# Weight blocks, outer sums and the first layer of the odd batches in a cross-attention and gated-MLP kernel

## The chip, the cores and the metric

The kernel runs on one core of one Trainium2 chip. A core has TensorE (PE; its weight loads are listed as PEld), VectorE (DVE), ScalarE (ACT), GpSimd (POOL) and SyncE (SP), which here issues most DMA transfers. The metric is the device time of one execution in microseconds (us), lower is better; a change is judged by the median of several runs.

## The reference

For each of 8 batches and 8 heads, 512 tokens read 32 state rows by softmax attention, and the state rows read the tokens the same way. The results are concatenated over the 544 rows, the heads are joined to rows of 512 features, and a gated MLP follows, with h times cos(h) as its gate.

```
scores = scale * x @ state.T;   a  = softmax(scores);    xread = a  @ state
scores2 = scale * state @ x.T;  a2 = softmax(scores2);   sread = a2 @ x
rows = concat([xread, sread], axis=2)  ->  (8*544, 512)
h = rows @ w_in          # w_in  512 x 2048
out = (h * cos(h)) @ w_out   # w_out 2048 x 512
```

The weights of the MLP are given in double precision and are turned to float32 on the chip.

## The kernel before

**Steps.** The work is written as one list of steps, and every engine's instructions follow that order. A step is one tile of 128 of the 2048 hidden features for the 512 tokens of one batch: 16 steps a batch, 128 steps for the token rows, then 16 for the state rows of all batches. Two batches are a pair of 32 steps. A step has a phase: 0 and 1 are the first and last eight tiles of the even batch, 2 and 3 those of the odd one.

**First layer.** The kernel never forms `xread`. It multiplies the state by the weights first (L329, kept by ACT as `sw`, L462) and then by the softmax weights `aT`. `hidden` (L491) does it for one tile with two matmuls of 512 columns. From batch 2 on two tiles are taken together, and in phases 0 to 2 the 2 x 2 blocks of the pair are multiplied with seven products of 256 columns instead of eight (`seven_part`, L541). For that POOL makes four sums of `sw` blocks (`sw_sums`, L524) three steps ahead, DVE makes four half sums of `aT` once a batch (`halves`, L510), ACT copies two partial results (L544, L545), and DVE adds two halves afterwards (`seven_sum`, L550). Which tiles take this form is decided in `seven` (L501).

**Gate.** ACT rounds h to whole turns (`gate`, L561), DVE takes the distance (`gate2`, L564), ACT the sine (`gate3`, L567), DVE the product (`gate4`, L581), which writes g into one of twelve buffers ("quads") of four tiles in `g_all`. A quad is taken from the front of a list and put at its end when it is free.

**Second layer.** Each pair of batches against both halves of `w_out` is again seven products (`Product`, L710), and each product is seven stages of four matmuls (L760). A stage reads one 128 x 512 weight block out of a ring of four, which SP fills from DRAM (`fetch_block`, L698). The sums of g that the seven products need are the outer sums (L707 from `outer_sum`, step numbers in a table, L1085), the sums inside a product are POOL's (`Product.sums`, also L707). The first pair's even batch is an exception: it is multiplied with the plain weights in SBUF.

**First pair.** Steps 0 to 31 also convert the weights (ACT L244 and L247, DVE L250 and L253, POOL L258), run the second batch's attention, and make the weight blocks: `w_out` is four matrices a11, a12, a21, a22. Three outer weight sums (L1105 on DVE, L1148 on POOL) form the other matrices, four POOL sums of quarters per matrix (`inner_weights`, L674) form its blocks, and 8 blocks per matrix are stored to `blocks_kept` (L678): the four quarters themselves ("raw") and four sums. a22's own blocks are not made there: the matrix is copied to a DRAM tile `kept` in four transfers (L1110, step 17), fetched back at steps 41 to 44, and its sums and stores follow at steps 46 to 50; a12's at steps 51 to 55 (`late_weights`).

Of the kernel before, what the change touches and what calls it, by code (L numbers as in the profile page):

```python
# [22 lines left out]
def kernel(  # L23
# [67 lines left out]
    kept = spare.tile([QT, P, S], F32)  # L91
# [409 lines left out]
    def seven(t):  # L501
        return t.pair is not None and t.b > 1 and t.phase < 3
# [161 lines left out]
    def inner_weights(which, m, temps, pieces=range(4), at_step=None):  # L664
# [11 lines left out]
        def send(i):  # L676
            block = (m11, m12, m22, m21, t4, t1, t2, t3)[i]
            nc.sync.dma_start(  # L678
                out=blocks_kept[which, (0, 1, 3, 7, 2, 4, 5, 6)[i]].rearrange(
                    "p (i d) -> p i d", d=P),  # L680
                in_=block)

        if at_step is None:
            for i in range(4 if 3 in pieces else 0):
                send(i)
                stores_due.append(lambda i=i: send(4 + i))
        else:
            for i in range(8):
                weights_at[at_step + (i + 1) // 2].append(
                    lambda i=i: send(i))  # L690
# [366 lines left out]
    stage_at, sums_at, outer_at, weights_at = [defaultdict(list)  # L1057
                                               for _ in range(4)]
# [26 lines left out]
    for n in range(B // 2):  # L1085
        end = n == B // 2 - 1
        for r, engine, o, x1, x2, half in (
                ((25, 26), dve, 0, 2, 0, 0),
                ((27 - (not n), 28 - (not n)), dve, 0, 2, 0, 1), ((31, 31), pool, 2, 3, 2, 0), ((33, 33), dve, 0, 3, 0, 0),
# [4 lines left out]
            for i in range(2):  # L1094
                outer_at[PERIOD * n + r[i]].append(
                    (engine, n, o, x1, x2, half, i))
# [10 lines left out]
    def move(to_dram, q, i):  # L1107
        sb = quad(q)[:, i]
        o, x = (kept[i], sb) if to_dram else (sb, kept[i])
        nc.sync.dma_start(out=o, in_=x)  # L1110

    late_quads = []

    def late_weights(step):
        if step == 41:
            late_quads.append(quads_free.pop(0))
        if step < 45:
            move(False, late_quads[0], step - 41)
        if step == 46:
            late_quads.append(quads_free.pop(0))  # L1120
            inner_weights(2, matrix(late_quads[0]), quad(late_quads[1]),
                          at_step=step)
        elif step == 51:
            quads_free.append(late_quads[0])
            inner_weights(1, a12, quad(late_quads[1]), at_step=step)
        elif step == 56:
            quads_free.extend([A12, late_quads[1]])
# [17 lines left out]
    def pool_sum():  # L1145
        for i in range(QT):
            o, x1, x2 = [quad(q)[:, i] for q in (SQ, A21, A22)]
            nc.gpsimd.tensor_tensor(o, x1, x2, op=ALU.add)  # L1148

    for at_, what in (  # L1150
            (15, lambda: quads_free.append(10)),
            (16, pool_sum),
            (17, lambda: quads_free.append(9)),
            (17, lambda: inner_weights(3, matrix(SQ), temps[1])),
            (20, lambda: inner_weights(5, matrix(A21), temps[0])),
            (23, lambda: inner_weights(4, matrix(A22), temps[1])),
            (23, lambda: quads_free.append(A11)),
            (25, lambda: quads_free.append(A21)),
            (25, lambda: inner_weights(6, matrix(SQ), temps[0])),
# [4 lines left out]
    for step in (41, 42, 43, 44, 46, 51, 56):  # L1164
# [21 lines left out]
    def first_pair(step, t):  # L1186
# [13 lines left out]
        else:  # L1200
# [9 lines left out]
            go(3)  # L1210
            if step == 1:
# [9 lines left out]
        gate4(t)  # L1221
        if last >= 0 and 4 < step < 11:
# [3 lines left out]
        if step == 6:  # L1226
            states_kept(1, side_banks[0])
# [133 lines left out]
```

## Time and profile before

| | |
|---|---|
| median of 12 runs | 760.3 us (757.62 to 761.71) |
| the profiled execution | 759.69 us, of which the span is 757.9 us |
| granted TensorE clock in it | 0.993 |
| PE waited longest for | DVE's gate product at L491: 11.7 us in 10 waits |
| SP waited longest for | PE's L760 before a ring fetch: 302.0 us in 128 waits |
| largest groups | POOL L707 337.5 us, PE L760 344.9 us, PE L491 110.4 us |

A row of the timeline has start, duration, engine, line, operation, written tile, read tiles, the number of instructions, and in brackets the idle time before them and what ended it. An fp32 matmul appears as two records. Line numbers are those of the kernel before.

### The profile page before, as it was taken

To read this page: it belongs to the slowest core of one execution; us is meant where nothing else is said; L and a number is where in the kernel's file an instruction comes from. 1 tells how busy PE (TensorE), PEld (TensorE's weight loads), DVE (VectorE), ACT (ScalarE), POOL (GpSimd) and SP (SyncE) were. 2 spreads that over 40 slices of the span, in tenths; PEclk is the share of its full clock that TensorE was granted. 3 is DMA by queue.
4 is the path that set the end of the run, shared out by engine and by line. 5 is a ranking of instruction groups with operands and counts; after the bars stand their busy time and mean duration, and the time that the engine had idled before them with its cause. 6 is when DMAs were issued, how large, how long until landed. Compare 5 with 4: busy or idle time off the path is not lost.

```text
span 757.9 us, 10478 instructions
## 1 busy us (share of the span) xinstructions
PE 721.4 (95%) x3552; PEld 507.3 (67%) x3552; DVE 493.7 (65%) x685; ACT 330.4 (44%) x538; POOL 514.5 (68%) x476
## 2 busy tenths in 40 slices
PE   8999889789999989999999999999999999999998
PEld 3443323347777866677768776677778767888886
DVE  5768789785974647676867666859746446264650
ACT  3877963634363435344454454443634432211110
POOL 2343477676998975387998853579989534799600
PEclk9999999999999999999999999999999999999999
DMA  8595479767235894576326843672324456445661
GB/s 249 167 268 176 154 167 305 249 148 173 83 96 135 183 263 157 112 155 139 87 67 143 181 107 89 146 173 81 85 69 112 122 171 151 114 153 177 182 158 40
DMA packets 211509, 113.42 MB, mean 150 GB/s; under 512 B 158400, under 2 KB 173248, under 8 KB 211456
## 3 DMA queue, kind: packets, MB, share of 16 engines
q1 hardware_dynamic: 210368, 112.23, 57.2%
q8 instruction: 28, 0.46, 0.3%
q10 hardware_dynamic: 960, 0.39, 0.2%
q14 instruction: 25, 0.20, 0.1%
q0 software_dynamic: 128, 0.13, 0.1%
HBM read 88.08 MB, written 24.64 MB: 149 GB/s over the span
## 4 chain that ended last, share of the span: by engine, by line
PE 55%; POOL 18%; DVE 2%; issue 2%; DMA 1%; ACT 1%; POOLq 0%; DVEq 0%
PE o L760 30%; POOL g_all L707 14%; PE h L491 9%; PE h L541 9%; PE at L861 2%; PE at L329 2%; POOL swS_all L524 2%; POOL sw L524 1%; PE at L426 1%; DMA g_all<-blocks_kept 1%; PE o L861 1%; DVE g_all L707 1%; DVE xT L311 1%; DVE q_all L564 0%; ACT q_all L567 0%
## 5 line engine op out<-in xcount | busy, mean ns | idle before, releaser
L707 POOL TENSOR_TENSOR g_all<-g_all 128x512 f32<-128x512 f32 x256 | 337.5, 1350 | 109.8 <-PE o L760 62.6
L760 PE MATMUL o<-g_all 128*128 128x256 f32 x1456 | 344.9, 382 | 4.8 <-DMA g_all<-blocks_kept 2.4
L760 PEld LDWEIGHTS o<-g_all 128*128 128x128 f32 x1456 | 273.7, 190 | 65.8 <-issue 15.3
L491 PE MATMUL h<-aT,sw 128*128 128x512 f32 x224 | 110.4, 617 | 12.4 <-DVE g_all L581 11.7
L564 DVE TENSOR_TENSOR q_all<-q_all,h 128x1024 f32<-128x1024 int32 (+1 forms) x88 | 85.4, 971 | 51.4 <-ACT q_all L561 51.3
L567 ACT ACTIVATE q_all<-q_all,halfpi 128x1024 f32<-128x1024 f32 (+1 forms) x88 | 84.1, 956 | 64.0 <-DVE q_all L564 63.9
L581 DVE TENSOR_TENSOR g_all<-h,q_all 128x1024 f32<-128x1024 f32 (+1 forms) x88 | 85.8, 975 | 39.3 <-ACT q_all L567 37.1
L561 ACT ACTIVATE q_all<-h 128x1024 int32<-128x1024 f32 (+1 forms) x88 | 73.2, 831 | 67.3 <-DVE g_all L581 34.2
L491 PEld LDWEIGHTS h<-aT,sw 128*128 128x128 f32 x224 | 41.6, 193 | 59.4 <-issue 31.8
L550 DVE TENSOR_TENSOR h<-h,sums_all 128x256 f32<-128x256 f32 x72 | 30.9, 429 | 63.0 <-PE h L541 48.3
L707 DVE TENSOR_TENSOR g_all<-g_all 128x1024 f32<-128x1024 f32 x40 | 56.9, 1439 | 0.1
L541 PE MATMUL h<-aS_all,swS_all 128*128 128x256 f32 x144 | 45.8, 400 | 3.0 <-ACT sums_all L545 1.8
L541 PE MATMUL h<-aT,sw 128*128 128x256 f32 x144 | 45.2, 396 | 3.3 <-DVE g_all L581 2.9
L765 ACT COPY o<-o 128x256 f32<-128x256 f32 x26 | 9.3, 357 | 86.6 <-PE o L760 86.6
L258 POOL TENSOR_TENSOR w_in<-w_in,aS_all 128x1024 int32<-128x1024 int32 (+1 forms) x10 | 19.3, 1929 | 39.1 <-DVE w_in L253 23.7
L541 PE MATMUL h<-aS_all,sw 128*128 128x256 f32 x144 | 43.6, 384 | 0.0
L771 ACT COPY o<-sums_all 128x256 f32<-128x256 f32 x26 | 9.8, 377 | 74.2 <-PE o L760 74.2
L604 DVE SCALAR_TENSOR_TENSOR held<-o,held 128x512 f32<-128x512 f32 x40 | 27.1, 681 | 21.3 <-PE o L760 20.8
L541 PEld LDWEIGHTS h<-aS_all,swS_all 128*128 128x128 f32 x144 | 25.6, 191 | 22.5 <-POOL g_all L707 8.3
L462 ACT COPY sw<-at 128x512 f32<-128x512 f32 x50 | 26.8, 588 | 31.2 <-PE at L329 31.2
L258 POOL TENSOR_TENSOR g_all<-g_all,aS_all 128x1024 int32<-128x1024 int32 x8 | 18.9, 2366 | 23.6 <-DVE g_all L253 11.2
L541 PEld LDWEIGHTS h<-aT,sw 128*128 128x128 f32 x144 | 26.2, 191 | 13.1 <-DVE g_all L581 9.8
(115 smaller groups left out, 878.9 us busy)
## 6 DMA issues: line engine op xcount, KB each, us to landing
g_all<-blocks_kept SPq DMA_DIRECT2D x202, 256.0 KB, 2.8
blocks_kept<-g_all SPq DMA_DIRECT2D x48, 256.0 KB, 3.4
g_all<-in_moe_w_out_dram SPq DMA_DIRECT2D x8, 1024.0 KB, 5.0
out_dram<-ot SPq DMA_DIRECT2D x128, 64.0 KB, 2.2
g_all<-in_moe_w_in_dram SPq DMA_DIRECT2D x6, 1024.0 KB, 5.3
xT<-in_x_dram SPq DMA_DIRECT2D x96, 64.0 KB, 3.0
x_b<-in_x_dram SPq DMA_DIRECT2D x24, 256.0 KB, 4.8
x_b<-in_x_dram SPq DMA_DIRECT2D x16, 128.0 KB, 4.4
```

What stands on the lines that cost most here:

```text
L258: nc.gpsimd.tensor_tensor(bits, bits, e, op=ALU.add)
L462: (copy or nc.scalar.copy)(sw_of[self.b, nt][:, j, c0:c1], to[j][:, c0:c1])
L491: nc.tensor.matmul(out=t.hp, lhsT=t.lhs(i), rhs=t.rhs(i), start=(i == 0), stop=(i == t.kn - 1))
L541: nc.tensor.matmul(out=out_, lhsT=w, rhs=r, start=start, stop=True, skip_group_check=True)
L550: nc.vector.tensor_tensor(o, h2[:, LO], sums_all[:, 0], op=ALU.add)
L561: nc.scalar.activation(t.q.bitcast(I32), t.hp, func=ACTF.Copy, bias=0.25)
L564: nc.vector.tensor_tensor(t.q, t.q.bitcast(I32), t.hp, op=ALU.subtract)
L567: nc.scalar.activation(t.q, t.q, func=ACTF.Sin, bias=halfpi, scale=-TWO_PI)
L581: nc.vector.tensor_tensor(g, t.hp, t.q, op=ALU.mult)
L604: nc.vector.scalar_tensor_tensor(out=out.t[:, ch], in0=bank, scalar=TWO_PI, in1=b.t[:, ch], op0=ALU.mult, op1=ALU.add)
L707: engine.tensor_tensor(o[:, i:i + n], x1[:, i:i + n], x2[:, i:i + n], op=ALU.subtract)
L760: nc.tensor.matmul(out=o, lhsT=ring[(self.first + k) % NB][:, i], rhs=g[:, i], start=(start and i == 0), stop=(i == QT - 1), skip_group_ch ...
```

## The change

1. `seven` has no bound on the phase any more: the last eight tiles of batches 3, 5 and 7 take the seven-product form.
2. The four POOL sums of a11's quarters go from steps 12 to 15 to steps 7 to 10. Raw blocks and sums are stored apart (`send_raw` and `send`); a11's raw blocks go at step 15, its sums at step 16.
3. The third outer weight sum, a22's place from the second sum minus a11, goes from DVE (steps 20 and 22) to POOL (step 18, four instructions). The fourth, DVE's, goes from steps 23 and 24 to 22 and 25.
4. a22's raw blocks are stored at step 17 in their final place, in place of the four copies to `kept`, and a12's at step 19. Step 41 fetches a22's four raw blocks at once; the late sums and stores, now four stores per matrix, begin at steps 45 and 52.
5. The outer sums of the first pair stand at steps 25, 26, 26 and 28 (before: 25, 26, 26, 27), and the first two of them between the distance and the gate product. The half sums for batch 2 stand in the same place at steps 29 and 30.
6. At step 6 the kept state rows (L172) come before a weight conversion.

```diff
     def seven(t):
-        return t.pair is not None and t.b > 1 and t.phase < 3
+        return t.pair is not None and t.b > 1
...
+    def send_raw(which, m, back=False):
+        for i, block in zip((0, 1, 7, 3), quarters(m)):
+            o, x = blocks_of(which, i), block
+            nc.sync.dma_start(out=x if back else o, in_=o if back else x)
...
-                ((27 - (not n), 28 - (not n)), dve, 0, 2, 0, 1), ...
+                ((27 - (not n), 28), dve, 0, 2, 0, 1), ...
...
+                at_ = mid_at if n == 0 and r[i] < 27 and r[0] == 25 else outer_at
...
         if step == 41:
             late_quads.append(quads_free.pop(0))
-        if step < 45:
-            move(False, late_quads[0], step - 41)
-        if step == 46:
+            send_raw(2, matrix(late_quads[0]), back=True)
+        elif step == 45:
             late_quads.append(quads_free.pop(0))
             inner_weights(2, matrix(late_quads[0]), quad(late_quads[1]),
-                          at_step=step)
-        elif step == 51:
+                          send_at=(49, 49, 50, 51))
+        elif step == 52:
...
-        weights_at[12 + i].append(lambda i=i: inner_weights(
-            0, a11, temps[0], (i,)))
-        weights_at[17].append(lambda i=i: move(True, A22, i))
+        weights_at[7 + i].append(lambda i=i: inner_weights(
+            0, a11, temps[0], (i,), () if i < 3 else (16,) * 4))
...
-            ((20, 22), A22, SQ, A11, ALU.subtract),
-            ((23, 24), SQ, A12, A22, ALU.subtract)):
+            ((22, 25), SQ, A12, A22, ALU.subtract)):
...
+            (15, lambda: send_raw(0, a11)),
+            (17, lambda: send_raw(2, a22)),
+            (19, lambda: send_raw(1, a12)),
...
+            (18, lambda: pool_sum(A22, SQ, A11, ALU.subtract)),
...
+            for what in mid_at[step]:
+                outer_sum(*what)
...
+        if step == 6:
+            states_kept(1, side_banks[0])
         if last >= 0 and 4 < step < 11:
             convert(last, "bcdf")
...
+        if t.b == 1 and s in (13, 14):
+            halves(2, s - 13)
```

On POOL in steps 5 to 18 of the kernel before, L258 are the conversions, L674 the sums of quarters and L1148 the first outer weight sum:

```order
L258 TENSOR_TENSOR g_all<-g_all,aS_all 128x1024 x3
L674 TENSOR_TENSOR g_all<-g_all 128x512
L258 TENSOR_TENSOR g_all<-g_all,aS_all 128x1024
L674 TENSOR_TENSOR g_all<-g_all 128x512
L258 TENSOR_TENSOR g_all<-g_all,aS_all 128x1024
L674 TENSOR_TENSOR g_all<-g_all 128x512
L258 TENSOR_TENSOR g_all<-g_all,aS_all 128x1024
L674 TENSOR_TENSOR g_all<-g_all 128x512
L1148 TENSOR_TENSOR g_all<-g_all 128x512 x4
```

In the changed kernel the same place reads as follows (L257 the conversions, L681 the sums of quarters, L1144 the two outer weight sums on POOL):

```order
L681 TENSOR_TENSOR g_all<-g_all 128x512
L257 TENSOR_TENSOR w_in<-w_in,aS_all 128x2x512
L681 TENSOR_TENSOR g_all<-g_all 128x512
L257 TENSOR_TENSOR g_all<-g_all,aS_all 128x1024
L681 TENSOR_TENSOR g_all<-g_all 128x512 x2
L257 TENSOR_TENSOR g_all<-g_all,aS_all 128x1024 x5
L1144 TENSOR_TENSOR g_all<-g_all 128x512 x4
L681 TENSOR_TENSOR aS_all<-g_all 128x512
L681 TENSOR_TENSOR aS_all<-aS_all,g_all 128x512
L681 TENSOR_TENSOR aS_all<-g_all 128x512
L681 TENSOR_TENSOR aS_all<-g_all,aS_all 128x512
L1144 TENSOR_TENSOR g_all<-g_all 128x512 x4
```

The four sums of a11's quarters stand between earlier conversions, and four instructions of the third outer weight sum stand behind the second matrix's quarters.

On DVE in steps 24 to 27 of the kernel before, L1105 is half of a weight sum, L707 half of an outer sum, L564 the distance and L581 the gate product:

```order
L1105 TENSOR_TENSOR g_all<-g_all 128x1024
L564 TENSOR_TENSOR q_all<-q_all,h_864 128x512
L581 TENSOR_TENSOR g_all<-h_864,q_all 128x512
L707 TENSOR_TENSOR g_all<-g_all 128x1024
L564 TENSOR_TENSOR q_all<-q_all,h_896 128x512
L581 TENSOR_TENSOR g_all<-h_896,q_all 128x512
L707 TENSOR_TENSOR g_all<-g_all 128x1024 x2
L564 TENSOR_TENSOR q_all<-q_all,h_913 128x512
L436 TENSOR_TENSOR sr<-at_118,i_616 32x128 x4
L581 TENSOR_TENSOR g_all<-h_913,q_all 128x512
L707 TENSOR_TENSOR g_all<-g_all 128x1024
```

In the changed kernel (L563 the distance, L580 the product, L709 an outer sum, L1108 a weight sum):

```order
L563 TENSOR_TENSOR q_all<-q_all,h_868 128x512
L709 TENSOR_TENSOR g_all<-g_all 128x1024
L580 TENSOR_TENSOR g_all<-h_868,q_all 128x512
L1108 TENSOR_TENSOR g_all<-g_all 128x1024
L563 TENSOR_TENSOR q_all<-q_all,h_901 128x512
L709 TENSOR_TENSOR g_all<-g_all 128x1024
L580 TENSOR_TENSOR g_all<-h_901,q_all 128x512
L709 TENSOR_TENSOR g_all<-g_all 128x1024
L563 TENSOR_TENSOR q_all<-q_all,h_918 128x512
L435 TENSOR_TENSOR sr<-at_117,i_617 32x128 x4
L580 TENSOR_TENSOR g_all<-h_918,q_all 128x512
```

Two outer sums stand between a distance and its product, step 24 has no weight sum, step 25 has one, and the sum of step 27 is gone from here.

On SP in steps 46 to 48 of the kernel before, L698 are ring fetches, L678 stores of blocks (512x1x128 a raw one), L132 loads of x and L623 stores of the output:

```order
L698 DMA g_all<-blocks_kept 128x512
L678 DMA blocks_kept<-g_all 512x1x128
L698 DMA g_all<-blocks_kept 128x512
L132 DMA xT<-in_x_dram 32x16x32 x4
L623 DMA out_dram<-ot 32x16x32 x4
L698 DMA g_all<-blocks_kept 128x512
L678 DMA blocks_kept<-g_all 512x1x128 x2
L132 DMA x_b<-in_x_dram 128x8x64 x4
L698 DMA g_all<-blocks_kept 128x512
L678 DMA blocks_kept<-g_all 512x1x128
L678 DMA blocks_kept<-g_all 128x512
```

In the changed kernel (L700 the fetches, L131 the loads, L622 the output, L684 stores of block sums):

```order
L700 DMA g_all<-blocks_kept 128x512 x2
L131 DMA xT<-in_x_dram 32x16x32 x4
L622 DMA out_dram<-ot 32x16x32 x4
L700 DMA g_all<-blocks_kept 128x512
L131 DMA x_b<-in_x_dram 128x8x64 x4
L700 DMA g_all<-blocks_kept 128x512 x3
L684 DMA blocks_kept<-g_all 128x512 x2
```

No raw store is left, and the first stores of sums stand behind more fetches.

More of the change, by code (lines that the diff above doesn't have):

```diff
@@ L676, in send @@
         def send(i):
[L677 to L686, printed above, removed]
-        else:
-            for i in range(8):
-                weights_at[at_step + (i + 1) // 2].append(
-                    lambda i=i: send(i))
+            nc.sync.dma_start(out=blocks_of(which, (4, 5, 6, 2)[i]),
+                              in_=(t1, t2, t3, t4)[i])
+        if send_at is None:
+            send_raw(which, m)
+            stores_due.extend([lambda i=i: send(i) for i in range(4)])
+        else:
+            for i, step in enumerate(send_at):
+                weights_at[step].append(lambda i=i: send(i))
     stage_list = []
@@ L1163 @@
         weights_at[at_].append(what)
-    for step in (41, 42, 43, 44, 46, 51, 56):
+    for step in (41, 45, 52, 57):
         weights_at[step].append(lambda step=step: late_weights(step))
@@ L1308 @@
             pd.sums(k)
[L1309 to L1311 removed]
+        if t.b < B - 1 and t.b > 1 and s in (12, 13):
+            halves(t.b + 1, s - 12)
         if 4 <= step < 4 + NH:
```

39 lines of the change are left out of this document (16 added, 23 removed).

## The prediction

> **What bounds the kernel now.** I read the page first (busy shares and the chain that ended last), then the windows by stretch, then the timeline of each engine where the stretches differ.
>
> ```profile
> PE 721.4 (95%) x3552; PEld 507.3 (67%) x3552; DVE 493.7 (65%) x685; ACT 330.4 (44%) x538; POOL 514.5 (68%) x476
> ...
> 120.00:160.00 40.00, 31.11 (x128) 12.74 (x125) 34.30 (x45) 17.35 (x29) 26.41 (x18) 0.96 0.87 270
> ...
> 200.00:240.00 40.00, 38.45 (x207) 30.38 (x208) 27.98 (x41) 19.79 (x33) 39.37 (x42) 1.00 0.37 104
> 240.00:280.00 40.00, 37.57 (x197) 29.15 (x196) 22.72 (x34) 15.02 (x26) 33.13 (x38) 0.96 0.90 206
> 280.00:320.00 40.00, 40.00 (x205) 27.33 (x205) 25.94 (x35) 19.43 (x30) 20.59 (x16) 1.00 0.57 151
> ```
>
> The first row gives each engine's busy time; the others are 40 us windows (span; busy us of PE, PEld, DVE, ACT, POOL; granted clock; DMA share; GB/s). TensorE is busy 95% of the span, so almost every us won must come off PE's own work or out of its 37 us of gaps. From 280 to 320 us PE is busy all 40.00 us and POOL 20.59: there PE is the bound and POOL has room. From 120 to 160 us PE is busy only 31.11 and DVE 34.30: there, in the first pair of batches, DVE sets the pace. From 200 to 240 us POOL is nearly full (39.37) and PE too (38.45). From 240 to 280 us PE lost 2.4 us and the granted clock was 0.96. The change touches three of these: the first pair (DVE), the last eight tiles of the odd batches (PE), and the late weight blocks around 250 to 270 us.
>
> **Part 1: the last eight tiles of batches 3, 5 and 7 take the seven-product form.**
>
> ```profile
> 297.51 1.72 PE h L491 x4
> ...
> 237.54 1.29 PE h L541 x6
> ...
> 242.87 0.45 POOL L524 TENSOR_TENSOR swS_all<-sw 128x128 f32<-128x128 f32 x1 [2.21 <-ACT sw L462]
> ...
> PE h L541 <- DVE g_all L581: 2.9, 7, 0.4
> PE h L541 <- ACT sums_all L545: 1.8, 4, 0.5
> PE h L541 <- POOL swS_all L524: 0.8, 3, 0.3
> ```
>
> The first two rows are pieces of the chain of waits (start, us, group, records): one fp32 matmul leaves two records, so a tile of two 512-column matmuls is the x4 of 1.72 us, and a pair of tiles 3.44. The seven products are 14 records of 256 columns at 1.29 / 6 = 0.215, or 3.01. Each pair of tiles saves 0.43 us, and 3 batches x 4 pairs = 12 pairs save 5.2. Four POOL sums of 0.45 us come with each pair; POOL has 20 idle us in that window, and the sums are queued three steps ahead, so I cost them at nothing. The two ACT copies and two DVE sums a pair are at nothing too, as ACT and DVE are busy 19.43 and 25.94 of these 40 us. If that cover went, PE would wait as it does now in the 36 pairs that already have this form: the last three rows (who waits for whom: us in total, times, longest) sum to 5.5 us, 0.15 a pair, so 1.8 for twelve. PE's gain is between 3.4 and 5.2; I take **4.6**, nearer the full value because these waits fall mostly where POOL is full.
>
> **Part 2: first pair, steps 6 to 16.** At step 6 the kept state rows move ahead of a weight conversion.
>
> ```profile
> 59.68 1.09 PE L329 MATMUL h<-w_in,st_all 64*32 64x512 f32 x16 [1.20 <-DVE st_all L172]
> ...
> 88.85 0.69 DVE L250 TENSOR_SCALAR g_all<-g_all 128x1024 int32<-128x1024 int32 x1 [0.35 <-ACT g_all L244]
> 89.57 1.23 DVE L253 SCALAR_TENSOR_TENSOR g_all<-g_all 128x1024 int32<-128x1024 int32 x1
> ...
> 93.28 1.27 POOL L674 TENSOR_TENSOR g_all<-g_all 128x512 f32<-128x512 f32 x1
> 93.48 1.62 DVE L250 TENSOR_SCALAR g_all<-g_all 128x1024 int32<-128x1024 int32 x1 [0.34 <-ACT g_all L244]
> ...
> 99.45 2.18 DVE L253 SCALAR_TENSOR_TENSOR g_all<-g_all 128x1024 int32<-128x1024 int32 x1
> ...
> 104.74 2.17 DVE L253 SCALAR_TENSOR_TENSOR g_all<-g_all 128x1024 int32<-128x1024 int32 x1
> ```
>
> PE waited 1.20 us for that DVE instruction, which two conversions held up; freed of them it runs about 1.9 us earlier, and the 1.2 goes (PE is dense for the next steps). The other rows are DVE conversions (L250, L253) alone and beside a POOL weight sum (L674): 0.69 becomes 1.62, and 1.23 becomes 2.18 and 2.17. Moving the four weight sums of the first matrix from steps 12-15 to 7-10 frees these three: 0.93 + 0.95 + 0.94 = 2.8, all on DVE's serial path, since the next gate distance follows each conversion. At steps 7 to 10 they meet other conversions. DVE has gaps there behind PE and ACT, so I charge one collision, 0.9 (bounds: none, and all of the 2.8). Sum: 1.2 + 2.8 - 0.9 = **3.1**, between 1.2 and 4.0.
>
> **Part 3: first pair, steps 16 to 30.** DVE's rows, step by step:
>
> ```profile
> 114.47 2.19 DVE L1105 TENSOR_TENSOR g_all<-g_all 128x1024 f32<-128x1024 f32 x1
> ...
> 123.78 1.20 DVE L1105 TENSOR_TENSOR g_all<-g_all 128x1024 f32<-128x1024 f32 x1
> ...
> 131.69 1.22 DVE L1105 TENSOR_TENSOR g_all<-g_all 128x1024 f32<-128x1024 f32 x1
> ...
> 137.88 1.27 DVE L1105 TENSOR_TENSOR g_all<-g_all 128x1024 f32<-128x1024 f32 x1
> ...
> 143.46 1.22 DVE L1105 TENSOR_TENSOR g_all<-g_all 128x1024 f32<-128x1024 f32 x1
> ...
> 146.06 0.69 DVE L581 TENSOR_TENSOR g_all<-h,q_all 128x512 f32<-128x512 f32 x1 [0.79 <-ACT q_all L567]
> 146.67 1.78 DVE L707 TENSOR_TENSOR g_all<-g_all 128x1024 f32<-128x1024 f32 x1
> ...
> 150.45 3.67 DVE L707 TENSOR_TENSOR g_all<-g_all 128x1024 f32<-128x1024 f32 x2
> ...
> 156.46 1.22 DVE L707 TENSOR_TENSOR g_all<-g_all 128x1024 f32<-128x1024 f32 x1
> ```
>
> L1105 is a half of a weight sum, L707 an outer sum, L581 the gate product; the bracket at L581 is 0.79 us in which DVE stood idle for ACT's sine. Start to start, a sum of 1.20 takes 1.13. Step 20 loses its half: -1.1. Step 22 trades one half for another, but POOL is now busy beside it, and the row at 114.47 shows such a half at 2.19: +1.0. Step 23 loses one, but ACT's table loads and exponentials set the next distance, so I count only -0.4. Step 24 loses one: -1.1. At step 25 an outer sum fills the 0.79 and no longer meets POOL, while a weight half comes in: -0.3. Step 26 has one sum in the 0.79 and one behind: -0.75. Step 27 loses its sum to step 28: -1.1. DVE gains 3.8 by the end of step 27. The first layer's half sums at steps 29 and 30 move into the sine gap too; I count nothing for them, since PE is dense from there.
>
> ```profile
> 132.98 1.28 POOL L674 TENSOR_TENSOR aS_all<-g_all 128x512 f32<-128x512 f32 x1 [4.41 <-DVE g_all L1105]
> ...
> 155.87 1.09 PE L329 MATMUL at<-w_in,st_all 64*32 64x512 f32 x16 [2.43 <-DVE sr L436]
> 156.90 3.68 PE L491 MATMUL h<-aT,sw 128*128 128x512 f32 x4
> ```
>
> PE enters that dense stretch after waiting 2.43 us for DVE at 155.87, and its next tile takes 3.68 us where 1.72 is usual. DVE's gain up to that point, without step 27, is 2.7; with the wait shortened to under 1.7 the slow tile may go (-1.9), so PE gains 2.7 to 4.6: I take **4.2**. The third sum costs POOL four more instructions of 1.28, about 5.1 us. They stand where POOL waited 4.41 us for DVE's third sum (first row) and after the 5.1 us of sums that left for steps 7-10, so I cost them at nothing. They also wait until the raw blocks of the same matrix have been read out; POOL works on eight other sums meanwhile. Uncovered, they make POOL 5.1 us later, and PE's gain here would be 2.7 - 5.1 = -2.4: the lower bound.
>
> **Part 4: late weight blocks, steps 41 to 57.** Eight raw stores disappear there (written in the first pair now, in place of four copies), and the reload comes as four transfers at once.
>
> ```profile
> 258.62 1.20 SPq L678 DMA_DIRECT2D blocks_kept<-g_all  x2
> 259.87 4.02 SPq L132 DMA_DIRECT2D x_b<-in_x_dram  x4
> 263.99 1.25 SPq L698 DMA_DIRECT2D g_all<-blocks_kept  x1
> ...
> 268.61 2.79 PE L760 MATMUL o<-g_all 128*128 128x256 f32 x8 [2.43 <-DMA g_all<-blocks_kept]
> ...
> 272.90 1.98 PE L760 MATMUL o<-g_all 128*128 128x256 f32 x8
> ...
> 216.18 10.85 POOL g_all L707 x8
> ...
> 379.17 10.86 POOL g_all L707 x8
> ...
> 537.36 10.85 POOL g_all L707 x8
> ```
>
> The first rows are SyncE's queue: two raw stores, a load of x, then the fetch of a weight block that PE needed. PE waited 2.43 us for it, and from 268.61 to 272.90 it took 4.3 us for twelve records that take 2.6 at 0.215: another 1.7. The same place in three pairs of batches (last rows: a POOL group of the chain) lies 163.0 us apart the first time and 158.2 the second: the pair with the late blocks costs 4.8 more. Without the two stores the fetch issues 1.2 us earlier into emptier queues, and later pairs, which have no such stores, show no such wait. I take **4.1** (2.43 + 1.7), between 1.2 (the issue time alone) and 4.8. SyncE has other moves to carry: the first pair issues 48 block stores where it issued 40 and four copies, so four more, 2.4 us by the first row's 0.6 each. They stand ahead of loads that are read some steps after; I cost them at nothing, and at 2.4 if a load came late. The four reloads at step 41 push one ring fetch back by as much, with three blocks in hand: nothing.
>
> On the 1.7: the Trainium skill's "TensorE: Matmul & The Clock Gate", Part 1, drops the clock only after an idle window of about 3.4 us; by it, removing the wait would give 2.4 and no more. Here eight records took 2.79 us after 2.43 us of idleness, so the measurement decides.
>
> **Sum.** 4.6 + 3.1 + 4.2 + 4.1 = 16.0 us. The profiled execution took 759.7 us (757.9 span and 1.8 around it), so 743.7; the median of the runs is 0.6 higher, so 744.3. I predict **744**. With all lower bounds, 3.4 + 1.2 - 2.4 + 1.2 = 3.4: 756.9; with all upper, 5.2 + 4.0 + 4.6 + 4.8 = 18.6: 741.7.
>
> **Rivals.**
>
> - *The first pair becomes POOL's.* The third sum's 5.1 us on POOL are not covered, and of 7.3 only 2.2 is left: 749.4. For it: everything that follows in the second layer reads sums of POOL. Against: the 4.41 us wait and the sums moved out of its way. Chance 0.22.
> - *The late fetch is still late.* It stands behind the 4.02 us load of x, which stays: only 1.2 of 4.1, 747.2. Against: the later pairs have that load too. Chance 0.14. Both together 752.3: 0.05.
> - *The seven-product tiles make PE wait.* POOL's and ACT's extra work comes late for PE, and the 4.6 is gone: 748.9. Against: the windows. Chance 0.05.
> - *Slower: DVE's queue stalls in the new tiles.*
>
> ```profile
> DVE h L550 <- PE h L541: 48.3, 38, 2.4
> ...
> 322.23 1.28 POOL L707 TENSOR_TENSOR g_all<-g_all 128x512 f32<-128x512 f32 x1 [6.76 <-DVE g_all L707]
> ```
>
> DVE adds the halves of a seven-product pair in order and stands still until PE has them: 48.3 us in 38 waits, 1.27 each, plus 0.43 of work. Eight more in each odd batch are 13.6 us in front of the outer sums for which POOL already waits 6.76 us at 322.23; POOL's own sums, and PE after them, would then start later. It costs something once the stalls exceed DVE's 14 idle us of that window, and beats all gains (11.4 elsewhere and PE's 5.2) if each of three odd batches loses over 5.5 us. At 6 each it would be 759.7 - 11.4 - 5.2 + 18, or 761. Against it: DVE's idle time. Chance 0.03.
>
> That the change does nothing it says can be left out: the orders of instructions show each move. Within 0.2% (1.5 us, about what a measurement of this kernel can tell from no change) would need nearly all terms to fail: 0.02.
>
> **How the numbers follow.** Forecast 0.49, the rivals 0.22, 0.14, 0.05, 0.05, 0.03, no change 0.02. The forecast's own range is 741 to 747; the two larger rivals lie at 747 to 749.5, so the range runs from 740.5 to 750.5 and leaves out the double failure, the last two cases and a little beyond the upper bound. Faster 0.95, same 0.02, slower 0.03.
>
> **What would show it.** Part 1: the stretches of batches 3, 5, 7 with the seven form are each 1.5 us shorter, PE still without gaps, and POOL busier there. Part 2: no conversion over 1.3 us between 93 and 107 us. Part 3: the 4.41 us wait of POOL gone, PE's 2.43 us wait under 1.7 and no tile of 3.7 behind it; PE's dense stretch starts about 7 us earlier. Part 4: no wait for a weight block near 264 us, and equal distances between the first and the later pairs. A new wait of POOL for transfers near 117 us, or a weight block that comes late to the first product, would make the prediction wrong.

## The result and the profile after

| | before | after |
|---|---|---|
| median of the runs | 760.11 us (32 runs, 757.51 to 761.71) | 744.17 us (8 runs, 743.76 to 745.32; a ninth run on record took 746.35) |
| ratio, 95% interval | | 0.9795, 0.9785 to 0.9806 |
| span of the profiled execution | 757.9 us | 742.3 us |
| granted TensorE clock in it | 0.993 | 1.000 |

The forecast was 744. Its sum came out right and two of its four terms did not; the rest of this document is about that. Line numbers here are those of the changed kernel, some lines off those of before: L328 is the state times weights (329 before), L490 a plain tile, L540 a seven-product tile, L762 a stage of the second layer, L709 an outer or inner sum of it, L1108 a weight sum on DVE, L249 and L252 the conversions, L681 a sum of quarters, L580 the gate product.

The page's first line and four windows of the kernel after, with the columns of the prediction:

```profile
PE 711.5 (96%) x3624; PEld 517.8 (70%) x3624; DVE 499.3 (67%) x707; ACT 338.8 (46%) x562; POOL 539.3 (73%) x528
```

```profile
120.00:160.00 40.00, 33.54 (x147) 16.20 (x147) 34.44 (x47) 21.28 (x37) 30.37 (x25) 1.00 0.89 264
...
200.00:240.00 40.00, 38.86 (x221) 30.05 (x220) 25.59 (x40) 20.66 (x35) 37.11 (x40) 1.00 0.49 119
240.00:280.00 40.00, 40.00 (x216) 31.50 (x216) 26.28 (x38) 17.38 (x32) 38.52 (x43) 1.00 0.75 186
280.00:320.00 40.00, 39.51 (x227) 31.44 (x226) 34.48 (x48) 21.50 (x36) 25.56 (x30) 1.00 0.56 126
```

PE is busy 10 us less, DVE 6 us more, POOL 25 more. The granted clock is 1.00 in all four windows; in the kernel before it was 0.96 from 120 to 160 and from 240 to 280. From 240 to 280 PE has no gap left (37.57 before). From 280 to 320 it has 0.49 us of gaps where it had none, and DVE went from 25.94 to 34.48 us.

To find where the 15.6 us of span come from I compared the starts of the same PE rows: the 16 records of "state times weights" occur at 41 places of each program, so the distance between two of them is free of when the program began.

| place (step) | before | after | won so far |
|---|---|---|---|
| first pair, step 7 | 59.68 | 58.51 | 1.2 |
| step 19 | 113.03 | 110.04 | 3.0 |
| step 24 | 132.71 | 127.57 | 5.1 |
| step 28, PE dense from here | 155.87 | 148.89 | 7.0 |
| step 32 | 179.20 | 170.58 | 8.6 |
| step 48, late blocks | 258.43 | 249.94 | 8.5 |
| step 51 | 275.68 | 262.81 | 12.9 |
| batch 3, step 60 | 322.65 | 307.70 | 15.0 |
| step 64 | 341.81 | 328.32 | 13.5 |
| step 83 | 434.30 | 420.43 | 13.9 |
| step 96 | 500.36 | 485.87 | 14.5 |
| batch 7, step 120 | 617.03 | 601.24 | 15.8 |
| first tile of the state rows (L491; L490) | 640.55 | 624.50 | 16.1 |

So the first pair gave 8.6 (forecast 3.1 + 4.2 = 7.3), the late blocks 4.4 (4.1), and the seven-product form about 2.8 (4.6): 0.6 in each of batches 3 and 5 and 1.5 in batch 7, whose last pairs stand behind the row of step 120. In batch 3 the table shows 2.1 us won at step 60 and 1.5 given back by step 64. Of these 1.5, 0.43 is no loss: at step 60 ten of the last pair's 14 records are still to come, where the plain form has half of its records behind it. The other 1.0 is a loss. Up to the last rows of PE and DVE the 16.1 stay; what follows them, the storing of the last output, takes some 0.5 us more in this profile, and 15.6 is left.

The rows of the timeline that answer to those of the prediction (the conversions and POOL of the first pair, the entry into the dense stretch, and SyncE's queue at the late blocks):

```profile
93.31 0.70 DVE L249 TENSOR_SCALAR g_all<-g_all 128x1024 int32<-128x1024 int32 x1 [0.34 <-ACT g_all L243]
98.36 1.22 DVE L252 SCALAR_TENSOR_TENSOR g_all<-g_all 128x1024 int32<-128x1024 int32 x1
102.69 1.23 DVE L252 SCALAR_TENSOR_TENSOR g_all<-g_all 128x1024 int32<-128x1024 int32 x1
...
129.48 1.26 POOL L681 TENSOR_TENSOR aS_all<-g_all 128x512 f32<-128x512 f32 x1
...
148.89 1.09 PE L328 MATMUL at<-w_in,st_all 64*32 64x512 f32 x16 [0.84 <-DVE sr L435]
149.91 1.98 PE L490 MATMUL h<-aT,sw 128*128 128x512 f32 x4
...
247.74 4.35 SPq L131 DMA_DIRECT2D x_b<-in_x_dram  x4
252.19 2.02 SPq L700 DMA_DIRECT2D g_all<-blocks_kept  x3
```

The three conversions that took 1.62, 2.18 and 2.17 us take 0.70, 1.22 and 1.23. POOL's fourth matrix starts without a wait (it was 4.41 us). PE waits 0.84 us (2.43) before the dense stretch, and the next tile takes 1.98 for its records where it took 3.68. The weight fetch at 252.19 follows the load of x at once, and no wait of PE for a weight block is left there. The POOL groups of the chain of waits, one per pair of batches:

```profile
207.57 10.86 POOL g_all L709 x8
...
365.31 10.86 POOL g_all L709 x8
...
522.87 10.84 POOL g_all L709 x8
```

They lie 157.74 and 157.56 us apart (163.0 and 158.2 before): the pair with the late blocks costs no more than the others now.

### The profile page after: what moved, and what is told of

It reads as the page before. It is cut to its first block, busy times and chain, and to the rows that moved or that the text cites. A ratio compares the mean times of both kernels' runs of the same rounds, so it can differ in the third digit from the quotient of the medians.

```text
span 742.3 us, 10759 instructions
## 1 busy us (share of the span) xinstructions
PE 711.5 (96%) x3624; PEld 517.8 (70%) x3624; DVE 499.3 (67%) x707; ACT 338.8 (46%) x562; POOL 539.3 (73%) x528
## 4 chain that ended last, share of the span: by engine, by line
PE 55%; POOL 24%; DVE 6%; DMA 4%; issue 4%; SPq 3%; ACT 3%; POOLq 0%; DVEq 0%; ACTq 0%
PE o L762 28%; POOL g_all L709 17%; PE h L540 12%; PE h L490 5%; POOL swS_all L523 3%; PE at L328 2%; PE at L863 2%; DMA x_b<-in_x_dram 2%; POOL sw L523 2%; PE at L425 2%; DVE g_all L709 1%; SPq L131 1%; PE o L938 1%; SPq L669 1%; PE o L863 1%
## 5 line engine op out<-in xcount | busy, mean ns | idle before, releaser
L709 POOL TENSOR_TENSOR g_all<-g_all 128x512 f32<-128x512 f32 x256 | 335.5, 1341 | 55.1 <-DVE g_all L709 40.1
L762 PE MATMUL o<-g_all 128*128 128x256 f32 x1456 | 344.0, 381 | 2.4 <-POOL g_all L709 2.4
L762 PEld LDWEIGHTS o<-g_all 128*128 128x128 f32 x1456 | 273.6, 190 | 49.3 <-issue 5.5
L563 DVE TENSOR_TENSOR q_all<-q_all,h 128x1024 f32<-128x1024 int32 (+1 forms) x88 | 85.5, 972 | 47.7 <-ACT q_all L560 47.5
L580 DVE TENSOR_TENSOR g_all<-h,q_all 128x1024 f32<-128x1024 f32 (+1 forms) x88 | 85.7, 974 | 27.0 <-ACT q_all L566 25.2
L549 DVE TENSOR_TENSOR h<-h,sums_all 128x256 f32<-128x256 f32 x96 | 41.2, 430 | 76.0 <-PE h L540 58.0
L490 PE MATMUL h<-aT,sw 128*128 128x512 f32 x128 | 61.6, 605 | 10.9 <-DVE g_all L580 10.3
L540 PE MATMUL h<-aS_all,swS_all 128*128 128x256 f32 x192 | 60.3, 396 | 3.2 <-ACT sums_all L544 1.8
L540 PE MATMUL h<-aT,sw 128*128 128x256 f32 x192 | 59.6, 392 | 3.8 <-DVE g_all L580 3.4
L709 DVE TENSOR_TENSOR g_all<-g_all 128x1024 f32<-128x1024 f32 x40 | 58.4, 1475 | 0.1
L540 PE MATMUL h<-aS_all,sw 128*128 128x256 f32 x192 | 58.0, 384 | 0.2
L540 PEld LDWEIGHTS h<-aS_all,swS_all 128*128 128x128 f32 x192 | 33.8, 189 | 27.9 <-issue 11.4
L490 PEld LDWEIGHTS h<-aT,sw 128*128 128x128 f32 x128 | 22.8, 189 | 43.4 <-DVE g_all L580 19.3
L257 POOL TENSOR_TENSOR w_in<-w_in,aS_all 128x1024 int32<-128x1024 int32 (+1 forms) x10 | 19.3, 1928 | 36.9 <-DVE w_in L252 18.1
L540 PEld LDWEIGHTS h<-aT,sw 128*128 128x128 f32 x192 | 34.5, 189 | 16.3 <-DVE g_all L580 12.2
L523 POOL TENSOR_TENSOR swS_all<-sw 128x128 f32<-128x128 f32 x48 | 23.7, 494 | 29.0 <-ACT sw L461 29.0
L540 PEld LDWEIGHTS h<-aS_all,sw 128*128 128x128 f32 x192 | 35.6, 190 | 8.3 <-DVE h L549 2.8
L603 DVE SCALAR_TENSOR_TENSOR held<-o,held 128x512 f32<-128x512 f32 x40 | 27.2, 681 | 13.7 <-PE o L762 13.1
```

The costliest lines, as they stand in the source:

```text
L490: nc.tensor.matmul(out=t.hp, lhsT=t.lhs(i), rhs=t.rhs(i), start=(i == 0), stop=(i == t.kn - 1))
L523: nc.gpsimd.tensor_tensor(o, x1, x2, op=op)
L540: nc.tensor.matmul(out=out_, lhsT=w, rhs=r, start=start, stop=True, skip_group_check=True)
L549: nc.vector.tensor_tensor(o, h2[:, LO], sums_all[:, 0], op=ALU.add)
L563: nc.vector.tensor_tensor(t.q, t.q.bitcast(I32), t.hp, op=ALU.subtract)
L580: nc.vector.tensor_tensor(g, t.hp, t.q, op=ALU.mult)
```

## The experiments

All kernels but one are the changed kernel with an edit, so their medians stand against 744.17. They ran at other times and on three chips, where the kernel before took 759.0 to 759.5 instead of 760.1, so a difference of medians under about 1 us says little. Runs of one kernel spread by 1 to 2 us and more, part of it at the start (one profile is 1.5 us behind another by step 7) and part from a contest described at the end; the distances between PE rows in the profiles are the sharper measure, and the text gives both.

### The seven-product form

*Taken back in the changed kernel.*

```diff
-        return t.pair is not None and t.b > 1
+        return t.pair is not None and t.b > 1 and t.phase < 3
```

> The changed kernel, with the last eight tiles of batches 3, 5 and 7 back in the plain form; all else stays. By the prediction's step (0.43 a pair, 4.6 for twelve pairs) it takes 4.6 us more than the changed kernel: 748.8. By the distances between landmarks in the two traces (0.6 won in batch 3, 0.6 in batch 5, 1.1 in batch 7) it takes only 2.4 more: 746.6. If the form's twelve pairs won nothing at all, 744.2.

Measured: 747.59 us (747.05 to 748.55), 3.4 more. In the profile the stretches of steps 51 to 64 and 83 to 96 are 0.62 us longer each, and that of batch 7, up to the first tile of the state rows, 1.52: 2.8. Two short stretches elsewhere are 0.25 longer each. Here the form was worth 2.8 to 3.4, not 4.6.

*Alone in the kernel before.* The same edit, the other way round.

> The kernel before, with the seven-product form in those tiles as the only edit. The prediction's 4.6 gives 755.5; the 2.4 read from the traces gives 757.7. The loss of about 1.1 us in batches 3 and 5 should be seen here as well, as a wait of TensorE for the gate product in step 61, since nothing of the other parts stands there.

Measured: 754.24 us against 759.44 for the kernel before on the same chip, ratio 0.9939 (0.9925 to 0.9952): 3.6 to 5.7 us less, more than expected. Its profiled span is only 3.1 shorter, with 0.62 in each of the two stretches and 1.52 in batch 7, as in the changed kernel, and PE's wait of 0.42 for the gate product is there at the same place (327.67). The medians alone would sooner have confirmed the 4.6; it is the distances that refute it. The profiled run is the slowest of the five (756.54, the others 753.90 to 755.85), and what made the others faster no trace shows.

What gave the gain back shows in the timeline of the changed kernel at step 60 and 61, DVE's rows and then PE's:

```profile
309.94 0.43 DVE L549 TENSOR_TENSOR h<-h,sums_all 128x256 f32<-128x256 f32 x1 [0.53 <-ACT sw L461]
310.28 1.22 DVE L709 TENSOR_TENSOR g_all<-g_all 128x1024 f32<-128x1024 f32 x1
311.41 0.42 DVE L509 TENSOR_TENSOR aS_all<-aT 128x256 f32<-128x256 f32 x1
311.87 1.37 DVE L509 TENSOR_TENSOR aS_all<-aT,aS_all 128x256 f32<-128x256 f32 x1
313.16 0.68 DVE L603 SCALAR_TENSOR_TENSOR held<-o,held 128x512 f32<-128x512 f32 x1
313.76 0.42 DVE L549 TENSOR_TENSOR h<-h,sums_all 128x256 f32<-128x256 f32 x1
314.09 1.21 DVE L580 TENSOR_TENSOR g_all<-h,q_all 128x1024 f32<-128x1024 f32 x1
...
314.23 0.70 PE L540 MATMUL h<-aS_all,sw 128*128 128x256 f32 x2
315.36 0.70 PE L540 MATMUL h<-aT,sw 128*128 128x256 f32 x2 [0.42 <-DVE g_all L580]
```

DVE's queue is in order. At 309.94 it has stood 0.53 us ahead of a tile sum (L549); PE's records at 309.25, of the same pair, end at 309.84 (the row names ACT's copies, which end at that time too). Only then come an outer sum (L709), two half sums for the next batch (L509), a result (L603), the second tile sum and, at 314.09, the gate product. PE needs that product before it may write the tile's bank again: two of its records start 1.13 us after the two before them instead of 0.43.

*All half sums behind the gate product.*

```diff
-        if t.b < B - 1 and t.b > 1 and s in (12, 13):
-            halves(t.b + 1, s - 12)
+        if t.b < B - 1 and t.b > 1 and t.b % 2 and s == 13:
+            halves(t.b + 1, 0)
+            halves(t.b + 1, 1)
+        if t.b < B - 1 and t.b > 1 and not t.b % 2 and s in (12, 13):
+            halves(t.b + 1, s - 12)
```

> The changed kernel, with the two half sums that stand ahead of the gate product of step 13 in batches 3 and 5 (for the next batch's first layer) moved behind it, beside the other two. Theory: the gate product there waits behind VectorE's queue, and TensorE for it; 1.75 us of queue (0.46 and 1.30) leave, and each of the two batches wins back most of its 1.1 us: 742.2, with the distance between the two POOL groups of outer sums about 1 us shorter than 157.7. Rival one: the outer sum and the halves of the pair itself are what holds the gate product (batch 7, which has no such half sums, lost 0.6 too), so about half of it: 743.2. Rival two: the lost time has nothing to do with VectorE's queue (the form's POOL sums, or matmuls of 256 columns after which PE stands): 744.2. Rival three: the four half sums together then come late for the next batch's first tile at step 64 and TensorE waits there: 745 or more.

Measured: 744.93 us (744.22 to 745.08), 157.96 between the POOL groups: nothing won. Rows of its timeline (DVE, PE, POOL):

```profile
312.70 1.21 DVE L580 TENSOR_TENSOR g_all<-h,q_all 128x1024 f32<-128x1024 f32 x1
...
315.12 0.67 PE L540 MATMUL h<-aS_all,swS_all 128*128 128x256 f32 x2 [0.21 <-DVE aS_all L509]
320.82 0.67 PE L540 MATMUL h<-aS_all,sw 128*128 128x256 f32 x2 [0.57 <-POOL swS_all L523]
...
314.65 5.68 POOL L709 TENSOR_TENSOR g_all<-g_all 128x512 f32<-128x512 f32 x4
```

The gate product did come 1.4 us earlier (1.3 against the PE row of step 60) and PE's wait for it went. But the half sums were now late for PE (0.21), and POOL, whose four-sum group at 314.65 follows DVE's outer sum, was late with the weight sums (0.57). Three limits lie within 1 us of each other. The theory was neither shown nor refuted by this run; the next two decide.

*Outer sum ahead of the tile sum, half sums left.*

```diff
+                early_ = r[i] < 27 and r[0] == 25 if n == 0 else r[i] == 28
...
             if even:
+                for what in mid_at[step]:
+                    outer_sum(*what)
                 seven_sum(first, 0)
```

> The changed kernel, with only the second edit of the run that cleared VectorE's queue: the outer sum of step 12 in the odd batches goes ahead of the tile sum that waits for TensorE, and all half sums stay where they are. The sum fills the 0.53 us in which VectorE stood idle there, so POOL gets it 0.9 us earlier and the gate product comes 0.5 us earlier. If the two limits (VectorE's queue ahead of the gate product, POOL's sums behind the outer sum) are the whole of the loss, TensorE wins 0.4 to 0.6 in each of batches 3 and 5, half of what both edits together win: 743.1, with 157.2 between the POOL groups. If POOL's sums alone were the limit, all of it: 742.2 and 156.7. If the half sums alone were, nothing: 744.2 and 157.7.

Measured: 743.46 us (743.11 to 744.02); 157.35 and 157.19 between the groups, 0.4 less each: a part of the loss, as for two limits. *With two of the half sums also moved forward:*

```diff
         elif not even:
             gate4(t.mate)
+        if t.b in (3, 5) and s == 11:
+            halves(t.b + 1, 0)
...
-        if t.b < B - 1 and t.b > 1 and s in (12, 13):
+        if t.b < B - 1 and t.b > 1 and s in (12, 13) and (s == 13 or
+                                                          t.b % 2 == 0):
             halves(t.b + 1, s - 12)
```

> The changed kernel, with VectorE's queue cleared ahead of the gate product of step 13 in batches 3 and 5: two of the four half sums go two steps earlier, behind the gate product of step 11 (where VectorE stood idle for 1.03 us), the other two stay behind that of step 13, and the outer sum of step 12 goes ahead of the tile sum that waits for TensorE. The run with all four half sums behind step 13 has shown two limits: the gate product went 1.4 us earlier and TensorE's wait of 0.42 for it went, but then TensorE waited 0.21 for the half sums and 0.57 for POOL's weight sums at 320.8. Theory: the 1.0 us that each odd batch loses there is VectorE's queue, with POOL's outer sums behind it as the next limit; with both earlier, batches 3 and 5 win 0.9 to 1.0 each, the distance between the two POOL groups falls from 157.7 to 156.7, and the kernel takes 742.2. Rival: another limit (the sine, the copies) takes their place at once: 744.2 and 157.7.

Measured: 741.45 us (741.39 to 742.42), ratio 0.9770 to the kernel before (0.9746 to 0.9795); all its runs lie below all of the changed kernel's. The stretch from step 60 to 64 takes 19.59 us (20.62), in batch 5 19.60 (20.62), and the groups lie 156.67 and 156.47 apart.

```profile
304.35 0.41 DVE L509 TENSOR_TENSOR aS_all<-aT 128x256 f32<-128x256 f32 x1
304.80 0.43 DVE L509 TENSOR_TENSOR aS_all<-aT,aS_all 128x256 f32<-128x256 f32 x1
...
310.01 1.22 DVE L709 TENSOR_TENSOR g_all<-g_all 128x1024 f32<-128x1024 f32 x1
...
313.49 1.21 DVE L580 TENSOR_TENSOR g_all<-h,q_all 128x1024 f32<-128x1024 f32 x1
...
315.11 0.59 PE L540 MATMUL h<-aT,sw 128*128 128x256 f32 x2
315.54 0.59 PE L540 MATMUL h<-aS_all,swS_all 128*128 128x256 f32 x2
```

The half sums fill a gap after the gate product of step 59, the outer sum fills the 0.53, and PE's records are 0.43 us apart again. So 1.0 us in each of batches 3 and 5 was DVE's order, with POOL's sums behind it, and the form is worth 2.8 + 2.1 = 4.8 (rounded from 2.76 and 2.05) of the full 5.2 once it is put right. This kernel is faster than both.

### The late weight blocks

*The eight raw stores written once more in the late steps.*

```diff
+            raw_again(2, matrix(late_quads[0]), (46, 47, 47, 48))
...
+            raw_again(1, a12, (52, 53, 53, 54))
```

> The changed kernel, with the eight raw stores of the two late matrices put into the late steps again (46 to 48 and 52 to 54), where they write once more what is there already. If the stores ahead of a weight block's fetch are what made it late before, TensorE waits some 2.4 us for a block near 255 us and is slow for some records after it, and the kernel takes 4.6 us more: 748.8. If the four copies at steps 41 to 44 (now four transfers in one step) or the order of the fetches did it, there is no such wait and at most the 1.2 us of two issues: 744.2 to 745.4.

Measured: 749.04 us (746.39 to 751.93), 4.9 more; the stretch from step 48 to 51 is 4.9 us longer in the profile. SyncE's queue and PE there:

```profile
251.46 1.24 SPq L1114 DMA_DIRECT2D blocks_kept<-g_all  x2
...
256.95 1.09 SPq L700 DMA_DIRECT2D g_all<-blocks_kept  x1
258.08 0.52 SPq L1114 DMA_DIRECT2D blocks_kept<-g_all  x1
258.70 1.12 SPq L700 DMA_DIRECT2D g_all<-blocks_kept  x2
...
261.46 2.53 PE L762 MATMUL o<-g_all 128*128 128x256 f32 x8 [2.98 <-DMA g_all<-blocks_kept]
265.48 2.25 PE L762 MATMUL o<-g_all 128*128 128x256 f32 x8
```

Two stores (L1114) stand ahead of the load of x (252.74) and one between the fetches (L700), PE waits 2.98 us for a block, and its records after it take 2.53 and 2.25 us for eight, where 1.89 is usual. The four-at-once fetch of step 41 is in this kernel too, so the stores are the cause, not the copies. The size is less certain than the place: the five runs spread over 5.5 us.

### The first pair

Three edits undo one move each: the sums of a11 back to steps 12 to 15 (`weights_at[7 + i]` to `weights_at[12 + i]`), the state rows back behind the conversion, the third weight sum back on DVE.

> The changed kernel, with the first matrix's four inner sums back at steps 12 to 15. By the prediction's step (2.8 us of slow conversions, less 0.9 for a collision at steps 7 to 10) and by the two traces (2.83 us won between the gate products of steps 11 and 16, 0.99 lost between 7 and 11) it takes 1.8 to 1.9 more: 746.1; two or three conversions between 93 and 107 us take 1.6 to 2.2 us again, and one at 67 us becomes short. Rival: VectorE's lost time there is made good behind TensorE and ScalarE before TensorE's dense stretch, at 149 us: under 0.5, 744.2 to 744.7.

> The changed kernel, with the kept state rows of step 6 back behind the weight conversion. The prediction's term for them is 1.2 (TensorE's wait at 59.7 us comes back, and nothing makes it good): 745.4, with the gate product of step 16 1.2 us later, at 106.5. Rival: the collision that took 1.0 us at steps 7 to 10 is there only because VectorE came 1.2 us earlier beside the same POOL sum; then it goes with it, and the kernel takes 744.2 to 744.4, with the gate product of step 16 unchanged.

> The changed kernel, with the third weight sum back on VectorE (steps 20 and 22) and nothing else. VectorE gets two halves of 1.13 to 2.18 us back in its serial path, so TensorE's dense stretch, at 148.9 us, starts 2.3 to 4.4 us later: 746.5 to 748.6, and more if TensorE's wait there passes 1.7 us again and its next tile is slow (1.9). Rival: the sum was worth nothing there, and POOL, with 5.1 us less to do, is early for the first of the second layer's sums: 743 to 744.2.

```profile
92.02 1.63 DVE L249 TENSOR_SCALAR g_all<-g_all 128x1024 int32<-128x1024 int32 x1 [0.34 <-ACT g_all L243]
98.00 2.19 DVE L252 SCALAR_TENSOR_TENSOR g_all<-g_all 128x1024 int32<-128x1024 int32 x1
103.28 2.17 DVE L252 SCALAR_TENSOR_TENSOR g_all<-g_all 128x1024 int32<-128x1024 int32 x1
```

Sums at 12 to 15: 746.55 us, 2.4 more; the stretch from step 3 to 19 is 1.84 longer, and the slow conversions are back (rows above). State rows: 745.64 us, 1.5 more; the gate product of step 16 is at 106.52 (105.30), 1.2 later (between the PE rows of steps 3 and 19, 1.4). The collision did not go with them: the conversion of step 8 took 1.49 there (1.13 in the changed kernel). Third sum on DVE: 746.35 us, 2.2 more, a little under the 2.3 to 4.4 expected; the stretch from step 20 to 28 is 1.65 longer.

Three edits concern places between distance and gate product: the outer sums of steps 25 and 26 back at the end of their steps (`at_ = outer_at`), the last outer sum back from step 28 to 27 (`28 - (not n)`), and the half sums of steps 29 and 30 at the end (the `halves(2, s - 13)` of the diff removed, the call at the end of the step as before).

> The changed kernel, with the outer sums of steps 25 and 26 of the first pair back at the end of their steps instead of between gate distance and gate product. If they fill idle time there, VectorE falls behind by about 0.8 at step 25 and 0.75 at step 26, as the prediction has it: 745.0 to 745.7. If VectorE's time there is set by the sine's table and ScalarE anyway, 744.2.

> The changed kernel, with the last outer sum of the first pair back from step 28 to step 27. It stands behind the products that begin TensorE's dense stretch (148.9 us), so that start does not move. By the prediction (VectorE loses 1.1 us there, TensorE is dense from there) the kernel stays within 0.3 of 744.2. Rival: the next gate distances, and the half sums and POOL's weight sums behind them, come up to 1.1 us later and TensorE waits for them: 745.3. Rival the other way: POOL, which waits 1.23 us for this sum at 154.4 us, gets it earlier, and TensorE's 0.56 wait for POOL's weight sum goes: 743.6.

> The changed kernel, with the half sums of the first layer at steps 29 and 30 back at the end of their steps instead of between gate distance and gate product. The prediction counts nothing for them, as TensorE is dense from there: 744.2. Rival: the gate products there then leave the sine's 0.8 us empty twice, VectorE falls back by up to 1.6 us before the first seven-product tile at 155.2 us, and TensorE waits: 745 to 745.8.

Outer sums at the end: 746.90 us, 2.7 more; PE waits 3.11 us at the entry of the dense stretch, and step 24 to 28 is 2.0 longer (0.8 + 0.75 were expected; the two sums of step 26, with POOL at work beside them, also take 3.70 us for 3.46). Step 27: 745.03 us, 0.9 more; step 28 to 32 is 1.0 longer. Half sums at the end: 744.46 us, 0.3 more by the median, which the spread covers; step 28 to 32 is 0.72 longer in its profile. PE's rows of the last two:

```profile
151.93 1.99 PE L762 MATMUL o<-g_all 128*128 128x256 f32 x8 [0.56 <-DVE held L603]
154.66 1.98 PE L490 MATMUL h<-aT,sw 128*128 128x512 f32 x4 [0.73 <-DVE g_all L580]
```

```profile
158.60 0.67 PE L540 MATMUL h<-aS_all,swS_all 128*128 128x256 f32 x2 [1.30 <-DVE aS_all L509]
```

Each puts a wait for DVE (0.56 and 0.73; 1.30) into a stretch that I had called dense, in place of one of 0.56 for POOL in the changed kernel.

## Why the prediction was right, and where not

| part | forecast | measured between PE rows |
|---|---|---|
| 1, seven-product form | 4.6 | 2.8 |
| 2, first pair to step 16 | 3.1 | 3.0 |
| 3, first pair, steps 16 to 32 | 4.2 | 5.6 |
| 4, late blocks | 4.1 | 4.4 |
| elsewhere | 0 | -0.2 |
| sum | 16.0 | 15.6 |

**Part 1** failed in the step "The two ACT copies and two DVE sums a pair are at nothing too, as ACT and DVE are busy 19.43 and 25.94 of these 40 us." The 0.43 per pair was right: with DVE's order mended, batch 3 wins 1.65 us against the plain form, for four pairs. Batch 7, which has no half sums for a next batch, wins 1.5 as the prediction said; batches 3 and 5 win 0.6. But DVE's idle time is an average over the window; at step 60 its queue ran without a gap from 309.94 to 319 us, and the added tile sum brought a wait of 0.53 us into the queue ahead of the outer sum, the half sums and the gate product. That is the mechanism of the prediction's slower rival, which priced it at 6 us a batch; it cost 1.0. My fallback (0.15 of waits a pair, read from the 36 older pairs) could not see it, since none of those pairs has outer sums and half sums in one step.

**Part 2** came out in both pieces: state rows 1.2 to 1.4 (forecast 1.2), sums of quarters 1.84 (2.8 - 0.9 = 1.9).

**Part 3** was sized too small. Up to the dense stretch DVE won 4.0, not 2.7; 1.0 of that is the weight sum of step 18, 2.19 us beside POOL before and 1.18 now. In the kernel before, POOL was at work there already (four L1148 from 110.60 to 115.57); in the changed kernel the two begin together, and the contest described below, which 4 of 11 profiles lose, decides. So in this profile the 1.0 is in part luck; without it DVE won 3.0. The slow tile went, as hoped, which brings another 1.6 by step 32. That it would go with a wait under 1.7 us rests on no run: a wait of 1.84 (142.46, kernel before) and one of 3.11 (outer sums at the end) are each followed by a tile of 1.98. The prediction left the sum of step 27 out of this gain and counted nothing for the half sums of steps 29 and 30, "since PE is dense from there". The runs show that PE was dense only because those were out of the way: put back, they bring 1.0 and 0.7 of the 1.6 back as waits (the 0.7 in the profile; the median shows 0.3). The third sum was worth 1.65 alone and the first two outer sums 2.0. The rival of a first pair set by POOL (0.22) did not happen: the row at 129.48 shows that the sum lies where POOL used to wait.

**Part 4** was right in place and size; the store run returns it whole. The rival of a fetch that is late anyway (0.14) is refuted by the changed kernel itself: with the load of x alone ahead of it, the fetch is in time.

The sum was right because 1.8 too much in Part 1 met 1.4 too little in Part 3 and 0.3 in Part 4. Nothing in the prediction ties these errors together, and 1.0 of the 1.4 hangs on a contest: that the total fits is luck.

## What to carry to other kernels

Idle time of an in-order engine in a 40 us window is no cover for an instruction that waits: read the queue of the one step it joins, above all what stands behind it and who waits for that. A stretch in which the bottleneck is dense is dense only with its feeders as early as they are; price a moved instruction there by what is late next. When a wait goes and nothing is won, look for the second and third limit before dropping the theory: here three lay within 1 us; one edit alone won nothing, another alone 0.4, and only two moves together the 1.0.

## What the hardware showed

**A contest that turns on 10 ns.** At step 18 a DVE weight sum and a POOL sum of quarters start together. Rows of the changed kernel, and of the kernel with the outer sums at the end:

```profile
111.43 2.37 POOL L681 TENSOR_TENSOR aS_all<-g_all 128x512 f32<-128x512 f32 x1
...
111.47 1.18 DVE L1108 TENSOR_TENSOR g_all<-g_all 128x1024 f32<-128x1024 f32 x1
```

```profile
110.78 1.26 POOL L681 TENSOR_TENSOR aS_all<-g_all 128x512 f32<-128x512 f32 x1
...
110.83 2.29 DVE L1108 TENSOR_TENSOR g_all<-g_all 128x1024 f32<-128x1024 f32 x1
```

Where POOL began at most 0.04 us ahead (7 profiles of the changed kernel and its variants), DVE's sum took 1.18 and POOL's 2.35 to 2.37; where it began 0.05 ahead (4 profiles), POOL's took 1.26 or 1.27 and DVE's 2.29 or 2.30. (With the sums back at steps 12 to 15 the two do not begin together.) One of the two is held up for the whole of the other's instruction. PE takes 12.87 to 12.90 us from step 20 to 24 in the first case (14.02 with the third sum on DVE) and 13.86 to 13.88 in the second: 1.0 us of spread that belongs to no edit. The changed kernel's eight runs fall into 743.8 to 744.2 and 745.0 to 745.3; that the contest parts them is likely, but only one of them has a trace. That the two engines share a port which one of them holds for a whole instruction is what the Trainium skill's "SBUF — State Buffer", "Who interferes with whom", states; the 1.18 against 2.30 agree. It lets the one that issues first win, which at this distance the rows do not show: POOL begins first in both.

**The clock does not go by the length of the wait alone.** PE's 2.43 us wait at 155.87 in the kernel before and its 3.11 us wait at 151.24 in the kernel with the outer sums at the end stand at the same place. The second wait and the tile behind it, then windows of both, before first:

```profile
151.24 1.09 PE L328 MATMUL at<-w_in,st_all 64*32 64x512 f32 x16 [3.11 <-DVE sr L435]
152.26 1.98 PE L490 MATMUL h<-aT,sw 128*128 128x512 f32 x4
```

```profile
156.00:158.00 2.00, 2.00 (x18) 0.65 (x15) 2.00 (x3) 0.00 (x0) 0.66 (x2) 0.76 0.81 135
158.00:160.00 2.00, 2.00 (x4) 0.82 (x3) 1.47 (x3) 0.50 (x1) 1.09 (x1) 0.50 0.63 161
```

```profile
152.00:154.00 2.00, 2.00 (x12) 0.87 (x5) 1.70 (x3) 0.27 (x1) 2.00 (x2) 1.00 0.77 151
154.00:156.00 2.00, 2.00 (x10) 1.71 (x9) 1.46 (x2) 1.91 (x4) 0.30 (x1) 1.00 0.48 76
```

After the shorter wait the granted clock fell to 0.50, after the longer one it stayed at 1.00. The Trainium skill's "TensorE: Matmul & The Clock Gate", Part 1, lets the idle window run freely, so that its place counts; that fits, but the 2.43 is shorter than its window of about 3.4 us. What decided here stays open.
